# A landmark attention with a two-layer MLP on one core: from hand-woven generators to pieces of work ordered by an in-kernel list scheduler, with DMA transposes in turn with the loads and stores in four parts

## The chip, the cores and the metric

The kernel runs on one core of one Trainium2 chip. The metric is the device time of one execution in microseconds (us), the lower the better. A profile of one execution goes with each kernel; its span is the time from the first to the last instruction, some 2 us shorter than the device time of the same run. A run whose time is more than 1.5% above the fastest of the same kernel counts as slow; comparisons use fast runs only.

PE is TensorE's matmul, PEld its weight load, ACT is ScalarE, DVE is VectorE, POOL is GpSimd, SP is SyncE, which here only starts DMAs.

## The reference

The attention compares each of 576 tokens with 32 landmarks (means of 18 tokens each) instead of all tokens, for 8 batches of 8 heads; a two-layer MLP with Silu between its layers follows. Cut to what matters:

```python
q, k, v: (8, 8, 576, 64)            # batch, heads, tokens, head size
q_lm = q.reshape(B, H, 32, 18, D).mean(axis=3)      # k_lm likewise
A  = softmax(scale * q @ k_lm.T)     # 576 x 32
Bm = softmax(scale * q_lm @ k_lm.T)  # 32 x 32
C  = softmax(scale * q_lm @ k.T)     # 32 x 576
Z = Bm.T / (norm1(Bm) * norminf(Bm) + 1e-6)
for _ in range(6):
    Z = 2 * Z - Z @ Bm @ Z           # Newton's iteration for an inverse
x = (A @ Z @ C @ v)                  # heads side by side: (4608, 512)
h = x @ w_in                         # w_in (512, 2048)
return (h * sigmoid(h)) @ w_out      # w_out (2048, 512)
```

Both kernels fold Z, C, v and w_in into one matrix per batch, m = (Z C v) w_in, so that the first layer is A times m and its input never exists as such.

## The kernel before

All matmuls go through one helper, which is why most PE rows of its profile have line 60. Here are the parts that the change touches, with cuts marked.

```python
# landmark sums: 18 matmuls against an identity, 256 columns each
for j in range(J):
    mm(lmv, idb, qk[:, :, :, j, :], start=(j == 0), stop=(j == J - 1))
# transposes of q and k, on DVE, in 32x32 blocks
nc.vector.transpose(out=qT[:, 0, g]..., in_=qk[:, 0, g]...)
# landmarks spread over a block diagonal, so that a 128-row weight serves four heads
nc.vector.tensor_tensor(out=lmbd, in0=bc(lmT, 4, 2), in1=bc(hmask, 8, 1), op=OP.mult)
# scores of A and C: full 128-row products, most of whose weight is zero
mm(sa[:, hf, 0:HS2], LB(1, g, c), qT[:, 0, g, c, ...], start=(c == 0), stop=(c == 1))
mm(c_ps[0:VP, ...], kt[:, c, i], LB(0, g, c), start=(c == 0), stop=(c == 1))
# row sums of A: a product of 4 columns, reciprocal, a transpose, a product that spreads it
mm(csv[0:c1 - c0, ci, 4*g:4*g + 4], ets[g][:, c0:c1], honesb)
...
# first layer, with Silu as h/2 * (1 + tanh(h/2)): ACT does tanh, DVE the rest
mm(h_ps[:, hf, 0:HS2], m_t[b][:, g, dc*128:(dc+1)*128], etn_t[b][:, g, ...], ...)
nc.scalar.activation(out=sig, in_=h_ps[:, :, 0:HS2], func=AF.Tanh, scale=0.5)
nc.vector.scalar_tensor_tensor(out=gT[:, dc, o:o + S]..., in0=sig, scalar=1.0,
                               in1=h_ps[:, :, 0:HS2], op0=OP.add, op1=OP.mult)
...
# second layer; one store for all token rows of a batch that an output tile holds
mm(ops, gT[:, dc, c*128:(c+1)*128], w_out_sb[:, dc, :], start=(dc == 0), stop=(dc == NDC-1))
nc.scalar.activation(out=ost, in_=ops, func=AF.Copy, scale=0.5)
nc.sync.dma_start(out=out[b*S:(b+1)*S, :].rearrange("(l j) n -> j l n", j=J)[j:j+n],
                  in_=ost[p0:p0 + n * L, :])
...
# the order: attention is a generator with 26 stops, taken in equal steps between MLP units
for i, u in enumerate(units):
    want = (i + 1) * NST // len(units)
    while done < want:
        done += 1
        next(gen, None)
    u()
```

The softmax here doesn't subtract the row's maximum and nothing guards it: scores larger than these inputs give would overflow.

## Time and profile before

| | before |
|---|---|
| device time, median of 4 runs | 316.17 us (314.15 to 316.33) |
| span of the profiled run, mean granted clock | 312.8 us, 0.984 |
| PE, ACT, DVE, GpSimd busy | 90%, 53%, 66%, 10% |
| first matmul of the first layer | 34.9 us |
| last matmul starts | 305.0 us |

The prediction below shows the lines of the page and of the waits. One more view helps: the table of windows, which gives the length of each stretch, the busy time of each engine in it with the number of instructions in brackets, the granted clock, and the mean share of the 16 DMA engines that was busy (the times of the packets added up, so it can pass 1).

```profile
core 0: us, PE busy (x) PEld busy (x) DVE busy (x) ACT busy (x) POOL busy (x), PEclk, DMA share, GB/s
0.00:35.00 35.00, 16.16 (x175) 11.16 (x176) 26.15 (x60) 9.55 (x15) 15.92 (x30) 0.92 1.05 188
35.00:65.00 30.00, 25.55 (x241) 15.94 (x240) 26.19 (x53) 17.41 (x30) 4.93 (x8) 0.98 1.02 175
...
100.00:260.00 160.00, 159.05 (x1322) 91.31 (x1321) 109.34 (x223) 97.53 (x163) 8.02 (x13) 1.00 0.30 62
```

The reader is to see two things. In the first 35 us PE is busy for 16 while DVE is busy for 26. From 65 us on PE is busy nearly all the time, and the DMA engines have little to do: a share of 0.30 from 100 to 260 us. So there is room on DMA and GpSimd for work that PE and DVE do.

A busy PE isn't yet a PE at its rate: a matmul's row has its length with the pipeline in it (379 ns), while eight in a row start every 216 ns. So I call **PE work** the number of matmuls of each form times the distance at which that form follows itself in the trace, and for tiled forms one pass shared by the tiles that run at once. What is left of a stretch is **lost**; matmuls on zeros count as lost. Before: 253.0 us of work and 59.8 lost, of 312.8.

### The profile page before, as it was taken

The numbers are of one execution on the slowest core, as the hardware profiler recorded it, in microseconds if no ns is written. First come the engines' busy times: TensorE is split into PE (matmuls) and PEld (weight loads), VectorE is DVE, ScalarE is ACT, GpSimd is POOL, SyncE is SP. The second block draws the span as 40 slices with busy tenths as digits, with TensorE's granted clock in tenths as the row PEclk, the third lists the DMA queues.
The fourth block names the chain that finished last, engine by engine and source line by source line (L and its number), as shares of the span: only waits on it lengthen the run. The fifth ranks groups of instructions, "written<-read, shape, count | busy, mean of one in ns | idle before, by whom it ended". The sixth has DMA issues, their size and how long they took to land.

```text
span 312.8 us, 5645 instructions
## 1 busy us (share of the span) xinstructions
PE 280.7 (90%) x2268; PEld 161.9 (52%) x2268; DVE 207.4 (66%) x420; ACT 166.8 (53%) x277; POOL 32.0 (10%) x55
## 2 busy tenths in 40 slices
PE   0465889979999999999999999999999999999990
PEld 0443464546555654666455744665465644555440
DVE  6857689998988697579747794676448664555000
ACT  1042664775466665765475646565645757555110
POOL 7342302100210020102001020000000000000000
PEclk9998699999999999999999999999999999999997
DMA  6999999672528152193418261110111101121122
GB/s 116 210 209 207 206 210 209 86 147 69 96 50 151 56 91 56 45 161 62 83 55 145 73 90 46 52 24 16 35 55 36 44 11 45 47 47 56 52 77 75
DMA packets 18379, 28.16 MB, mean 90 GB/s; under 512 B 944, under 2 KB 9136, under 8 KB 18352
## 3 DMA queue, kind: packets, MB, share of 16 engines
q0 software_dynamic: 13600, 18.35, 34.6%
q1 hardware_dynamic: 4752, 9.44, 10.8%
q8 instruction: 18, 0.29, 0.4%
q14 instruction: 9, 0.07, 0.1%
HBM read 36.70 MB, written 9.44 MB: 147 GB/s over the span
## 4 chain that ended last, share of the span: by engine, by line
PE 72%; DVE 11%; DMA 8%; ACT 4%; issue 2%; POOL 1%; POOLq 0%; ACTq 0%
PE ops L60 36%; PE h_ps L60 18%; DVE gT L393 5%; DMA v_97<-in_v_dram 4%; PE lm_ps L60 3%; DMA w_in_sb<-in_moe_w_in_dram 3%; PE m_ps L60 3%; PE c_ps L60 2%; ACT sig L391 2%; PE w_ps L60 2%; PE sa_ps L60 2%; PE ns_ps L60 2%; DVE qT L171 2%; PE rb_ps L60 1%; ACT m L377 1%
## 5 line engine op out<-in xcount | busy, mean ns | idle before, releaser
L60 PE MATMUL ops<-w_out_sb,gT 128*128 128x512 bf16 x576 | 150.6, 379 | 0.1
L393 DVE SCALAR_TENSOR_TENSOR gT<-sig,h_ps 128x576 bf16<-128x576 bf16 x128 | 94.8, 746 | 53.2 <-ACT sig L391 53.0
L391 ACT ACTIVATE sig<-h_ps 128x576 bf16<-128x576 f32 x128 | 82.4, 651 | 56.9 <-PE h_ps L60 54.4
L60 PE MATMUL h_ps<-etn,m 128*128 128x288 bf16 x512 | 84.3, 287 | 3.4 <-DVE gT L393 2.6
L60 PEld LDWEIGHTS <-gT 128*128 128x128 bf16 x576 | 52.5, 98 | 44.3 <-issue 6.3
L60 PEld LDWEIGHTS <-m 128*128 128x128 bf16 x512 | 47.9, 98 | 34.6 <-issue 11.6
L377 ACT CAST m<-m_ps 128x1024 bf16<-128x1024 f32 x32 | 32.1, 1019 | 14.2 <-PE m_ps L60 14.1
L409 ACT ACTIVATE ost<-ops 128x512 f32<-128x512 f32 x36 | 21.4, 598 | 21.8 <-PE ops L60 21.6
L60 PE MATMUL lm_ps<-qk,idb 128*128 128x256 bf16 (+1 forms) x162 | 22.2, 289 | 6.3 <-DVE sel L127 6.3
L171 DVE STREAM_TRANSPOSE qT<-qk 128x576 bf16<-128x576 bf16 x32 | 23.8, 755 | 1.6 <-PE c_ps L60 1.6
L239 DVE SCALAR_TENSOR_TENSOR st<-st,ns_ps 128x320 bf16<-128x320 bf16 (+1 forms) x48 | 20.7, 432 | 5.5 <-PE ns_ps L60 5.4
L60 PEld LDWEIGHTS <-idb 128*128 128x128 bf16 x162 | 16.2, 112 | 11.2 <-issue 6.8
L166 DVE STREAM_TRANSPOSE qT<-qk 128x1152 bf16<-128x1152 bf16 x16 | 21.7, 1354 | 0.0
L304 ACT ACTIVATE ct<-c_ps 96x768 bf16<-96x768 f32 x16 | 12.9, 806 | 7.5 <-PE c_ps L60 7.5
L60 PE MATMUL ns_ps<-st 128*128 128x160 bf16 (+1 forms) x96 | 13.7, 223 | 2.1 <-DVE st L239 1.4
L60 PE MATMUL m_ps<-w_in_sb,zt 64*32 64x512 bf16 x256 | 13.8, 414 | 1.8 <-ACT m L377 1.0
L60 PE MATMUL c_ps<-lmbd,qT 128*96 128x128 bf16 x192 | 14.2, 219 | 0.2 <-ACT et L256 0.2
L60 PEld LDWEIGHTS <-qT 128*96 128x96 bf16 x192 | 13.3, 123 | 1.9 <-issue 0.4
L159 ACT CAST lm<-lm_ps 128x256 bf16<-128x256 f32 x8 | 3.0, 375 | 20.3 <-PE lm_ps L60 20.3
L290 DVE TENSOR_TENSOR etn<-et,rb_ps 128x576 bf16<-128x576 bf16 x16 | 12.0, 748 | 1.9 <-PE rb_ps L60 1.8
L256 ACT ACTIVATE et<-sa_ps 128x576 bf16<-128x576 f32 x16 | 10.4, 648 | 3.9 <-PE sa_ps L60 3.8
L73 POOL DMA_DIRECT2D qk<-in_k_dram x8 | 5.8, 720 | 62.3 <-PE lm_ps L60 45.4
(78 smaller groups left out, 171.4 us busy)
## 6 DMA issues: line engine op xcount, KB each, us to landing
out_dram<-ost SPq DMA_DIRECT2D x32, 256.0 KB
qk<-in_k_dram POOLq DMA_DIRECT2D x8, 576.0 KB, 5.6
qk<-in_q_dram POOLq DMA_DIRECT2D x8, 576.0 KB, 8.9
v_96<-in_v_dram POOLq DMA_DIRECT2D x12, 192.0 KB, 6.4
v_97<-in_v_dram POOLq DMA_DIRECT2D x12, 192.0 KB, 6.6
w_out_sb<-in_moe_w_out_dram POOLq DMA_DIRECT2D x4, 512.0 KB, 16.1
w_in_sb<-in_moe_w_in_dram POOLq DMA_DIRECT2D x2, 512.0 KB, 11.1
w_in_sb<-in_moe_w_in_dram POOLq DMA_DIRECT2D x4, 256.0 KB, 12.2
```

The source lines that it names most:

```text
L60: nc.tensor.matmul(out=out_ap, lhsT=lhsT, rhs=rhs, start=start, stop=stop, skip_group_check=True)
L73: nc.gpsimd.dma_start(out=qk[:, t].rearrange("p g j d -> p g (j d)"), in_=src[b].rearrange("(g h) (l j) d -> (h l) g (j d)", g=NG, l=L))
L166: nc.vector.transpose(out=qT[:, 0, g].rearrange("p c j l -> p j c l"), in_=qk[:, 0, g].rearrange("p j (c x) -> p j c x", c=2))
L171: nc.vector.transpose(out=qT[:, 1, g, c].rearrange("p (i a) l -> p a i l", a=VA), in_=qk[:, 1, g].rearrange("p (a i) (c x) -> p a i c x", ...
L239: nc.vector.scalar_tensor_tensor(out=st2[:, :, lo:SW], in0=st[:, :, lo:SW], scalar=2.0, in1=ns_ps[:, 0:NG * SW].rearrange("p (g x) -> p g ...
L256: nc.scalar.activation(out=et.rearrange("p (f x) -> p f x", f=2), in_=sa[:, :, 0:HS2], func=AF.Exp, scale=sc / J)
L290: nc.vector.tensor_tensor(out=etn[:, g, :].rearrange("p (f x) -> p f x", f=2), in0=ets[g].rearrange("p (f x) -> p f x", f=2), in1=rb[:, :, ...
L304: nc.scalar.activation(out=ct.rearrange("p (f x) y -> p f (x y)", f=2), in_=c_ps[0:VP, :, 0:384], func=AF.Exp, scale=sc / J)
L377: nc.scalar.copy(out=m_sb[:, :, f * 512:(f + 1) * 512], in_=m_ps)
L391: nc.scalar.activation(out=sig, in_=h_ps[:, :, 0:HS2], func=AF.Tanh, scale=0.5)
L393: nc.vector.scalar_tensor_tensor(out=gT[:, dc, o:o + S].rearrange("p (f x) -> p f x", f=2), in0=sig, scalar=1.0, in1=h_ps[:, :, 0:HS2], op ...
L409: nc.scalar.activation(out=ost, in_=ops, func=AF.Copy, scale=0.5)
```

## The change

The intent is to take work off PE and DVE, give it to DMA, GpSimd and ACT, and find an order in which nothing waits. Every piece of work (some matmuls, one copy, one load) becomes an object with a duration, what it depends on, a priority and the PSUM banks that it needs (PSUM holds what matmuls write, in eight banks). A list scheduler in the kernel's source goes through time and gives each engine the ready piece of the best priority. The order of instructions on each engine is then fixed.

The parts, beside the order:

- q and k are transposed by DMA from batch 2 on (by PE in batches 0 and 1); landmarks are summed by GpSimd from batch 2 on;
- scores of A and C run as 64-row by 32-column tiles, eight at once, without the block diagonal;
- row sums of A come from one product with a block of ones, which also spreads them; Ln and Exp on ACT take the reciprocal;
- C is computed with landmarks as rows, so its sums come out of the exponential; it is transposed by DMA (by PE in batches 0 and 1);
- Silu is one instruction on ACT, with a table load at each change between Silu and Exp;
- transposes wait until two of three v loads of the batch have landed, and loads wait for the transposes of the batch before;
- an output tile is stored by four DMAs of 64 KB;
- matmuls on zeros keep PE running in the first 45 us.

The diff, cut to its core:

```diff
+class Op:
+    def __init__(self, name, engs, emit, deps=(), prio=0.0, psum=0, cls=None, table=None,
+                 tiled=False, dma=0.0, lag=None, group=None, crit=False):
...
+class Plan:
+    LAG = {"PE": 0.24, "ACT": 0.17, "DVE": 0.12, "POOL": 0.2, "SP": 1.6}
+    MARGIN = 0.4
+    WARM = 45.0
...
+                    for o in cand[e]:
+                        r = o.ready + o.margin
+                        if r > t + 1e-9: ... continue
+                        if best is not None and o.prio >= best.prio:
+                            continue
+                        if e == "ACT" and o.table == "silu" and group[0] is not None:
+                            continue
...
+                    if e == "PE":
+                        if o.tiled != tiled[0]:
+                            dur += 0.08
...
+def act_us(n): return 0.06 + 0.00083 * n
+def dve_us(n): return 0.07 + 0.00104 * n
+def mm_us(n, count=1): return count * max(n / 2400 + 0.0025, 0.028)
...
-                nc.vector.transpose(out=qT[:, 0, g]..., in_=qk[:, 0, g]...)
+            gate = v_ops[b][-2:-1]
+                    qt_ops[t, g] = [A(f"xt{t}{g}.{b}", [("SP", 1.38)],
+                        lambda e, t=t, g=g: nc.sync.dma_start_transpose(
+                            out=qT[:, t, g], in_=qk[:, t, g].rearrange("p j d -> p (j d)")),
+                        [qk_ops[b, t]] + use + gate, p0 + 5, lag=XLAG)]
...
-                mm(lmv, idb, qk[:, :, :, j, :], start=(j == 0), stop=(j == J - 1))
+                xs = [pool(f"la{g}", 576, s1[:, g], src[:, g, 0:9], src[:, g, 9:18],
+                           [qk_ops[b, t], tree[0]]) for g in range(NG)]
+                x = pool("lb", 512, s2, s1[:, :, 0:4], s1[:, :, 4:8], xs)
+                x = pool("lc", 256, s1[:, :, 0:2], s2[:, :, 0:2], s2[:, :, 2:4], [x])
...
-                mm(sa[:, hf, 0:HS2], LB(1, g, c), qT[:, 0, g, c, ...], ...)
+            def am(e, g=g):
+                for h in range(4):
+                    for c in range(2):
+                        mm(bank(me[f"A{g}"], c)[L * h:L * h + L, 0:HS],
+                           lmT[64 * c:64 * c + 64, 1, g, L * h:L * h + L],
+                           qT[64 * c:64 * c + 64, 0, g, :, L * h:L * h + L])
...
-        nc.scalar.activation(out=sig, in_=h_ps[:, :, 0:HS2], func=AF.Tanh, scale=0.5)
-        nc.vector.scalar_tensor_tensor(out=gT..., in0=sig, scalar=1.0, in1=h_ps..., ...)
+                               lambda e, dc=dc, cell=cell: nc.scalar.activation(
+                                   out=gm[:, dc, :], in_=bank(cell["o"]), func=AF.Silu),
...
+    def later_loads(b):
+        p = last[b - 2]
+        gate = last[b - 1]["xts"][-2:-1] if b > NPE else []
+        if b - 2 >= NPE:
+            gate = gate + last[b - 2]["cts"][:1]
+        load_qk(b, 100.0 * b - 150, p["qk_read"], gate)
+        load_v(b, 100.0 * b - 149, [p["cv"]], gate)
...
-                    out=out[b*S:(b+1)*S, :].rearrange("(l j) n -> j l n", j=J)[j:j + n],
-                    in_=ost[p0:p0 + n * L, :])
+            eng.dma_start(
+                out=out[b*S:(b+1)*S, c0:c1].rearrange("(l j) n -> j l n", j=J)[j],
+                in_=ost[L * n:L * n + L, c0:c1])
```

## The prediction

> **What bounds the kernel now.** I read the page first: the line of busy time by engine, then the forty slices.
>
> ```profile
> PE 280.7 (90%) x2268; PEld 161.9 (52%) x2268; DVE 207.4 (66%) x420; ACT 166.8 (53%) x277; POOL 32.0 (10%) x55
> ...
> PE   0465889979999999999999999999999999999990
> PEld 0443464546555654666455744665465644555440
> DVE  6857689998988697579747794676448664555000
> ACT  1042664775466665765475646565645757555110
> ```
>
> PE is full from the tenth slice on; DVE is at eight or nine tenths in slices 7 to 13 and drops later. The waits agree: PE waits little for others, while ACT and DVE wait for PE.
>
> ```profile
> ACT sig L391 <- PE h_ps L60: 54.4, 63, 2.8
> DVE gT L393 <- ACT sig L391: 53.0, 57, 2.2
> ...
> PE lm_ps L60 <- DVE sel L127: 6.3, 1, 6.3
> ...
> PE h_ps L60 <- DVE gT L393: 2.6, 5, 1.2
> ```
>
> So the bound is PE, except at both ends. But busy PE is not PE at its rate, so I priced its work by spacing. The timeline shows "PE ops x8" in 1.73 us, 216 ns each; "h_ps x8" in 0.98 us, 123 ns; twelve c_ps in 0.67 us, 56 ns; nine lm_ps in 0.98 us, 109 ns; ten cs_ps of width 4 in 0.39 us, each lasting 164 ns, so 25 ns apart. A small matmul with a full weight load can therefore follow each 25 ns. Times the counts of these groups:
>
> ```profile
> L60 PE MATMUL ops<-w_out_sb,gT 128*128 128x512 bf16 x576 | 150.6, 379 | 0.1
> L60 PE MATMUL h_ps<-etn,m 128*128 128x288 bf16 x512 | 84.3, 287 | 3.4 <-DVE gT L393 2.6
> L60 PE MATMUL lm_ps<-qk,idb 128*128 128x256 bf16 (+1 forms) x162 | 22.2, 289 | 6.3 <-DVE sel L127 6.3
> L60 PE MATMUL c_ps<-lmbd,qT 128*96 128x128 bf16 x192 | 14.2, 219 | 0.2 <-ACT et L256 0.2
> ```
>
> second layer (ops) 576 x 0.216 = 124.4; first layer (h_ps) 512 x 0.1225 = 62.7; lm 15.7 (126 x 0.109 and 36 narrow ones at 0.056); c 10.7; sa 64 x 0.1225 = 7.8; m 256 in concurrent eights, 32 x 0.216 = 6.9; w 192 x 0.04 = 7.7; ns 6.0; sums and their spreading (cs, rt, rb) 8.0; the rest 2.8. **PE's work is 252.7 us of a 312.8 us span.** The other 60 us, from the counts in windows: 25 before the first h_ps at 35.1 us (about 10 us of work done by then); 12 in 35 to 100; 13 in 100 to 260 (8%, gaps between unlike pieces); 2 after; 7.4 from the last matmul at 305.4 to the end, for one copy and one store.
>
> The chain of waits in the first 36 us shows the start:
>
> ```profile
> 4.90 10.16 DMA w_in_sb<-in_moe_w_in_dram
> 15.34 13.71 DMA v_97<-in_v_dram
> 29.77 0.70 PE m_ps L60 x5
> 30.49 1.94 ACT m L377 x2
> 33.10 2.04 PE lm_ps L60 x9
> 35.13 0.96 PE h_ps L60 x4
> ```
>
> The timeline says more than the DMA labels: the landmark sums start only at 12.50, held by DVE's constants (two memsets of 2.62 us, then sel), and attention 0 runs serially from there, each of its Newton steps taking 0.9 us.
>
> **What the Trainium skill says.** "TensorE: Matmul & The Clock Gate", section "Back-to-back issue gap", gives N/2.4 + 2.5 ns warm: 216 ns at 512. The trace agrees (1.73 us for eight). "ScalarE: Activation LUTs", section "What ACT_TABLE_LOAD costs", gives 1283 ns plus a drain of 1380 per switch; the trace has one load, of 1.28 us, and no switch, so the drain is not seen here. "GPSIMD Engine Reference", section 3.1, measures about 2.6 cycles an element for a two-input add, at 1.2 GHz; no run here has one. "DMA: Bandwidth & Descriptors", section "Latency and other measured facts", has DMA transposes at 261 GB/s (350 to 400 contiguous); none here yet.
>
> **The change, part by part: PE.** Both layers keep their columns: the second 72 x 0.216 = 15.5 us a batch; the first becomes 32 matmuls of 512 and 32 of 64, 6.9 + 32 x 0.029 = 7.8. That is 23.4, as before. Attention, per batch, before and after:
> - landmark sums 2.0, now six adds per tensor on GpSimd (batches 0 and 1 stay on PE); four small transposes of the landmarks, 0.2, are added;
> - C scores 1.3 and A scores 1.0 become 64-row by 32-column tiles, eight at once: 0.25 each, say 0.5 with the change of tiling;
> - row sums 1.0 become four 288-column products with a block of ones, 0.5 (reciprocal by Ln and Exp on ACT);
> - C times V loses its ones columns: 192 to 128 columns, 1.0 to 0.7;
> - Newton 0.75, m 0.9 (say 1.1), zt and the rest 0.6.
>
> Sum after: 23.4 + 4.9 = about 28.3 a batch, against 31.6. Batches 0 and 1 pay 4.7 more each (36 sums, 36 transposes, 12 of C). **8 x 28.3 + 9.4 = about 235.5 us, 17 less than before.** Warm-up matmuls only fill time in which PE has nothing else.
>
> **DVE and ACT.** DVE loses its transposes (23.8 + 21.7 us), lmbd 5.5 and the 94.8 us of gT; what is fixed on it sums from the old rows to about 7 us a batch (chain and Newton 5.5, two etn at 0.75). ACT's Silu takes 18 x 0.60 = 10.8 us (the row of ost, 598 ns at 512 columns); exponentials and logarithms twelve of 288 columns at 0.40 and three others, 6.4; two table switches at 2.66, 5.3 by the skill: 22.5. Copies that either takes, 9. Together 38.5 over two engines, 19 each, under PE's 28: **neither is the bound on average**, though in an exponential stage Silu has to wait.
>
> **DMA and GpSimd.** Transposes move 128 x (4 x 1152 + 2 x 768) x 2 bytes = 1.57 MB a batch, 6 us at the skill's 261 GB/s (an estimate); loads 0.88 MB and stores 1.18 MB at the 207 GB/s of the page's early slices, 10. That is 16 us of some 29, even with loads and transposes in turn. GpSimd: 4608 elements at 2.2 ns, 10 us (an estimate from that page), and five load issues, 3.2 (rows of 720 and 588 ns): 13 of 29. Both hidden.
>
> **Start.** K lands near 7 us as now, q near 9; sums 1 us each, warm; landmark transposes, scores and the exponential with its table 3 to 4; the chain to f0 2; six Newton steps with the two groups in turn at 0.7, 4; zt, m and its copy 1.7. First h_ps near 22 instead of 35. The copies and transposes of batch 1 run beside this: about 12 us of work done, **10 lost instead of 25**. From 22 to 45 Silu of batch 0 (10.8 us against PE's 7.8) and w_out's late landing cost perhaps 5 (was 12).
>
> **Steady part.** Pieces of the second layer (four matmuls, 0.86 us) fill whatever attention leaves, and PE takes an attention piece only 0.4 us after it is ready. I take 5% lost of the remaining 218, 11 us; before it was 8%.
>
> **End.** The last block comes in two halves whose stores go out in four parts from two queues: 5 instead of 7.4.
>
> Sum: 235.5 + 10 + 5 + 11 + 5 = 266.5 us of span, and 3.4 for the difference between timed runs and span before (316.18 against 312.8): about 270. I add 2 for gaps at the many changes of tiling: **272 us**.
>
> **Rivals.** (1) ACT becomes the bound: its order is Silu or exponentials, never mixed, and no exponential stage may start with a first layer open. For it: 22.5 us fixed and up to 9 of copies is 31, above PE's 28, if DVE takes few; DVE is also quick to stall a chain. Against: the order is planned so that either engine takes a copy when free. It would make the period 31 to 33 us, and 290 to 300 in all. (2) Transposes with their turns arrive late: each batch passes load, wait, transpose, wait, and a fixed order can't step around a late one, so PE stands before the scores. For it: six transposes, five loads and eighteen stores share a period. Against: 16 of 29 us. At 2 us a batch for six batches: 284. (3) PE's old loss of 8% stays, as it comes of PE's own switching and not of order: 6 us more, 278. (4) The start is even better hidden and the steady loss 2%: 260.
>
> **Range and chances.** Work of 235 to 240 is the surest term; the losses of 20 to 50 us on top of it make the range: 258 to 289. For a result within 2% of now, 40 us of it would have to be given back by a new wait; chances 0.94 faster, 0.04 same, 0.02 slower.
>
> **What will show it.** PE's matmuls of 512 columns 216 ns apart; first first-layer matmul near 22 us (right: 19 to 25); PE idle in total under 20 us after that; ACT under nine tenths in the steady slices, with 16 or so table loads; DVE under half busy; the DMA share below eight tenths after slice 8; end of matmul to end of span about 5 us. Wrong would be: PE waiting for scores behind a transpose, ACT full while PE waits for Silu, or GpSimd adds several times longer than estimated, holding back the landmarks.

## The result

| | before | after |
|---|---|---|
| device time, median of 4 runs | 316.17 us | 276.88 us (274.86 to 277.45) |
| span, mean granted clock | 312.8 us, 0.984 | 275.0 us, 0.994 |
| PE work | 253.0 us | 228.4 us |
| lost in the span | 59.8 us | 46.6 us |
| first matmul of the first layer | 34.9 us | 30.7 us |
| last matmul starts, span ends | 305.0, 312.8 us | 270.5, 275.0 us |
| ACT, DVE, GpSimd busy | 53%, 66%, 10% | 64%, 35%, 39% |

The ratio of after to before is 0.876, with a 95% interval of 0.872 to 0.880. A ratio here is the mean time of one kernel's fast runs over that of the other's fast runs of the same rounds, so it isn't quite the ratio of the medians. The time is inside the predicted range of 258 to 289 us, 4.9 us above the predicted 272.0.

The page after, with the lines that answer to those of before:

```profile
PE 261.1 (95%) x2383; PEld 133.0 (48%) x2383; DVE 96.2 (35%) x261; ACT 176.4 (64%) x403; POOL 107.3 (39%) x133
...
PE   8999999997989989996999999999999999999993
...
ACT  1689697559884889985389898769881391111120
...
DMA  6999999999999899986999999543002321323223
```

PE is full from the first slice on, but the first slices are the matmuls on zeros. ACT works at eight or nine tenths in many slices of the middle, for at most five slices on end. DMA is near nine tenths to slice 25, where before it fell after slice 7. And in the last third ACT has little to do: the last product m starts at 198.6 us, so attention is through, and from 226 to 271 us only second layer is left.

Groups of instructions of after, by line, engine, form, count, then busy time and mean ns of one:

```profile
L811 ACT ACTIVATE gm<-ps 128x512 bf16<-128x512 f32 x128 | 67.0, 631 | 4.0 <-PE ps L323 3.7
...
L516 POOL TENSOR_TENSOR sa<-qk 128x576 f32<-128x576 bf16 x24 | 31.0, 1310 | 16.6 <-DMA qk<-in_k_dram 16.1
```

Silu takes 631 ns for 512 columns, one instruction in place of two. GpSimd's adds of 576 elements take 1310 ns, 2.27 ns an element. The second layer keeps its distance of 216 ns.

The waits, as engine and line, what it waited for, total us, times, longest:

```profile
POOL sa L516 <- DMA qk<-in_k_dram: 16.1, 6, 4.8
...
PE ps L323 <- DMA ct<-ce: 3.7, 2, 2.5
```

The chain that ended last, followed in order of time (start us, us, what); I show the start, the longer of two waits for a transpose of C, and the end:

```profile
6.35 14.56 DMA w_in_sb<-in_moe_w_in_dram
21.19 6.12 DMA w_in_sb<-in_moe_w_in_dram
...
126.14 2.73 DMA ct<-ce
...
171.54 93.59 PE ps L323 x655
...
269.28 1.62 DMA out_dram<-ost
```

Three things are to be seen. The first 27 us hang on w_in, which is still landing. Twice PE waits for a transpose of C (ct), 3.7 us in all. And from 171.5 us on the chain is PE alone for 94 us, up to the last copies and stores.

**Where the time came from.** By the same count of starts and distances, the span fell by 37.9 us, of which 24.6 are PE work and 13.2 are lost time:

| PE work, us | before | after |
|---|---|---|
| second layer and first layer | 187.1 | 187.3 |
| landmark sums (after: batches 0 and 1 only) | 15.7 | 4.0 |
| scores of A and C | 18.5 | 4.6 |
| row sums of A and their spreading | 8.0 | 3.9 |
| C times v | 7.7 | 5.1 |
| transposes of q, k, landmarks and C on PE | 0 | 7.1 |
| m, Newton and the rest | 16.0 | 16.4 |

| lost, us | before | after |
|---|---|---|
| to the first matmul of the first layer | 25.7 | 17.7 |
| from there until attention is through (after: 200 us, before: 260) | 26.1 | 23.6 |
| from there to the last matmul | 0.3 | 0.8 |
| last matmul to the end of the span | 7.8 | 4.5 |

The landmark sums and the transposes were tried by runs below. The scores, whose work fell most, the row sums and Silu as one instruction were not: their part is a count from the traces.

The middle hardly gained: after loses 14% of it. I sorted it by what stands at each gap of PE, with each pass of the tiles charged whole. From 45 to 200 us of after, some 11 of 22.5 us are 110 gaps at a change between untiled and tiled matmuls (or between two tilings), 6.9 us are four waits of over 0.6 us each, and the other 4 or so are small gaps within and between pieces of the same tiling. In the middle of before, 112 changes cost some 12 us, other gaps 10 and waits 4.0. So the order did part of what it was to do, and took more than half of the gaps between like pieces away; changes cost as much as before in a shorter middle, and waits grew. Between full and 64-by-32 matmuls a change costs 0.09 us on the way to the tiles and 0.10 on the way back: from the last tile of 512 columns to the next full matmul are 0.318 us, of which its pass takes 0.216, and for 288 columns 0.225, of which 0.122.

### The profile page after: what moved, and what is told of

It reads as the page before. It is cut to its first block, busy times and chain, and to the rows that moved or that the text cites. A ratio compares the mean times of both kernels' runs of the same rounds, so it can differ in the third digit from the quotient of the medians.

```text
span 275.0 us, 6159 instructions
## 1 busy us (share of the span) xinstructions
PE 261.1 (95%) x2383; PEld 133.0 (48%) x2383; DVE 96.2 (35%) x261; ACT 176.4 (64%) x403; POOL 107.3 (39%) x133
## 4 chain that ended last, share of the span: by engine, by line
PE 71%; DMA 11%; ACT 9%; DVE 3%; POOL 2%; issue 2%; SPq 0%; POOLq 0%; ACTq 0%; DVEq 0%
PE ps L323 71%; DMA w_in_sb<-in_moe_w_in_dram 8%; ACT gm L811 4%; DMA ct<-ce 2%; DMA out_dram<-ost 1%; POOL qk L368 1%; ACT m L333 1%; ACT L923 1%; DVE bm L570 1%; ACT ln L658 1%; ACT ost L333 1%; DVE etn L667 1%; POOL v L375 1%; ACT gx L834 1%; DVE m L335 0%
## 5 line engine op out<-in xcount | busy, mean ns | idle before, releaser
L323 PE MATMUL ps<-w_out_sb,gm 128*128 128x512 bf16 x512 | 121.8, 381 | 0.0
L323 PEld LDWEIGHTS <-gm 128*128 128x128 bf16 x512 | 47.4, 98 | 52.4 <-issue 3.5
L811 ACT ACTIVATE gm<-ps 128x512 bf16<-128x512 f32 x128 | 67.0, 631 | 4.0 <-PE ps L323 3.7
L323 PE MATMUL ps<-etn,m 128*128 128x64 bf16 (+1 forms) x512 | 69.3, 286 | 0.0
L516 POOL TENSOR_TENSOR sa<-qk 128x576 f32<-128x576 bf16 x24 | 31.0, 1310 | 16.6 <-DMA qk<-in_k_dram 16.1
L620 DVE SCALAR_TENSOR_TENSOR st<-st,ps 128x320 bf16<-128x320 bf16 (+3 forms) x54 | 21.4, 405 | 20.2 <-PE ps L323 18.3
L335 DVE CAST m<-ps 128x512 bf16<-128x512 f32 x32 | 20.3, 685 | 9.7 <-PE ps L323 9.7
L516 POOL TENSOR_TENSOR sb<-sa 128x512 f32<-128x512 f32 (+1 forms) x24 | 21.9, 912 | 1.9
L333 ACT CAST m<-ps 128x512 bf16<-128x512 f32 x32 | 17.5, 609 | 3.5 <-PE ps L323 3.4
L323 PE MATMUL ps<-w_out_sb,gx 128*128 128x512 bf16 (+1 forms) x80 | 16.3, 336 | 0.3 <-ACT ost L333 0.3
L667 DVE TENSOR_TENSOR etn<-et,ln 128x576 bf16<-128x576 bf16 x16 | 14.3, 893 | 1.8 <-ACT ln L662 1.8
L323 PEld LDWEIGHTS <-st 128*128 128x128 bf16 x96 | 8.1, 98 | 10.3 <-DVE st L620 1.1
## 6 DMA issues: line engine op xcount, KB each, us to landing
v<-in_v_dram POOLq DMA_DIRECT2D x24, 192.0 KB, 10.7
```

Source lines behind the costliest of these rows:

```text
L323: nc.tensor.matmul(out=out_ap, lhsT=lhsT, rhs=rhs, start=start, stop=stop, skip_group_check=True)
L333: nc.scalar.copy(out=out, in_=in_)
L335: nc.vector.tensor_copy(out=out, in_=in_)
L516: lambda e: nc.gpsimd.tensor_tensor(out=o_, in0=a_, in1=b_, op=OP.add),
L620: nc.vector.scalar_tensor_tensor(out=s2[:, g0:g1, lo:SW], in0=s[:, g0:g1, lo:SW], scalar=2.0, in1=ps[:, 0:NG * SW].rearrange("p (g x) -> p ...
L667: nc.vector.tensor_tensor(out=etn[:, g, :], in0=et.rearrange("p c x -> p (c x)"), in1=ln.rearrange("p c x -> p (c x)"), op=OP.mult)
```

## The experiments

My theory after the result had four parts. PE's work is still the price of nearly everything. The order is what keeps the moved work from stalling PE. Transfers are now close behind as a second limit, so the turns and the four-part stores matter. The changes of tiling are a true cost, about 0.11 us each. The rivals: that attention's own pace through the transfers is the bound and PE only fills the time; that any sensible order would do; that the turns and four-part stores are decoration, as DMA had room before; that the gaps at the changes are only waits for data put down wrongly.

Every run was correct except the first, which is wrong. Ratios are to the kernel before in the same rounds; after stands at 0.876.

### Half the second layer (wrong result)

```diff
-                    mm(ps, src(dc), w_out_sb[:, dc, c0:c1], start=(dc == 0), stop=(dc == NDC - 1))
+                    if dc % 2 == 0:
+                        mm(ps, src(dc), w_out_sb[:, dc, c0:c1], start=(dc == 0), stop=(dc == NDC - 2))
```

> Half of the second layer's matmuls left out (a wrong result on purpose): 288 of 576 at 216 ns, 62 us of PE work. If PE's work alone sets the time of the changed kernel, 277 falls by 62 to about 215 us. If the attention stages have a pace of their own (24 us a batch from 30 to 200 us in the trace, the DMA queues nine tenths busy), the last first-layer piece still comes near 215 to 225 us and the total stays at 225 to 235 us.

Measured: 235.95 us, ratio 0.747 (0.744 to 0.750). It skips half the second layer, 62 us of PE work, and returned 41. PE lost about 45 us between 30 and 180 us instead of 22 (up to 5 of it matmuls missing from the trace, 25 of 2087): there the other 21 went. The page has the slices of PE and DMA:

```profile
PE   8999999977799888899986588899998999999990
...
DMA  5999999999999999897987996999897630112554
```

PE shows fives to eights in many slices of the middle, and DMA is near nine tenths to slice 29. What says most is the start of m in the eight batches: 25.1, 58.6, 90.7, 105.9, 140.1, 154.2, 185.1 and 198.6 us in after, and 25.8, 55.5, 88.7, 104.2, 140.9, 154.9, 186.2 and 199.4 here. Attention goes at the same pace with a good part of PE's other work gone. So attention has a pace of its own in this order (whether transfers or dependences set it isn't shown), and PE's second layer fills what it leaves. What doesn't fit is done afterwards: that is the pure second layer at after's end. The rival that attention's pace is the bound is wrong for after, where some 70 us of PE's work are left when attention is through. But work taken out doesn't pay in full either: here a third of it came back as idle PE in the middle, though some 17 us of second layer and 8 of first were still left after attention. The time, 236 us, is at the upper end of the second expectation, 225 to 235.

### All transposes and landmark sums back on PE

```diff
-    NPE = 2
+    NPE = 8
```

(With it, two dependences that the reuse of buffers then needs, and the condition under which later loads are made.)

> All eight batches take their transposes and landmark sums on PE, none by DMA transpose or GpSimd: 6 x 84 more matmuls of 128 columns at 56 ns, 28 us of PE work more, and no turn-taking of transfers. If PE's work sets the time: 277 + 28 less the 7 us of long waits = 298 to 305 us. If the attention's pace through DMA and GpSimd cost PE more than those waits, the loss is smaller: 280 to 292 us. DVE's bm (404 ns) and etn (893 ns) should fall back to the 224 and 748 ns of the kernel before if it is GpSimd's adds that slow them.

Measured: 299.81 us, ratio 0.950 (0.946 to 0.955), 22.9 us above after. The edit adds 28 us of PE work (36 sums, 36 transposes and 12 of C in each of six batches). Waits of over 0.6 us fell from 6.9 to 1.6 us in the middle, so about 5 came back. The time followed PE's work nearly one for one: the first part of the theory holds. The same run settled a side question, as it has no GpSimd adds at all. One group of DVE, in after first and then in this run:

```profile
L570 DVE TENSOR_TENSOR bm<-pb,pbs 128x64 bf16<-128x64 f32 x8 | 3.2, 404 | 0.3
```

```profile
L570 DVE TENSOR_TENSOR bm<-pb,pbs 128x64 bf16<-128x64 f32 x8 | 1.8, 223 | 0.2
```

Without GpSimd's adds this instruction is as fast as in the kernel before (224 ns). The product etn goes from 893 to 753 ns likewise (748 before). So the adds slow DVE beside them. In after two of the eight bm instructions ran beside an add: they took 0.57 and 1.31 us, and each ended 0.08 us after its add did, as if it had waited for the add's end. The other six took 0.225.

### No turns between transposes and loads

```diff
-            gate = v_ops[b][-2:-1]
+            gate = []
```

(And the same in the loads and in the transposes of C.)

> The turns of transfers taken away: transposes and loads may run at once, only the buffers' own dependences stay. If the turns are what made attention wait (POOL waited 19 us for transposes, SP 37 us for v): 2 to 6 us faster, 271 to 275. If transposes beside loads get slower by more than the turns cost: landings over 3.6 us (transposes of qT) and 2.8 us (ct), same or slower, 277 to 285. If PE's work hides both: within 1 us.

Measured: 290.18 and 292.12 us in its two fast runs, ratio 0.922 (0.915 to 0.929); two more runs, 297.8 and 299.4, count as slow. That is about 15 us above after, on the fast runs. The view of the tile qT on SP gives the time from issue to landing as least, median and most, after first and then this run:

```profile
DMA to landing us min/median/max: 3.3/3.6/5.0
```

```profile
DMA to landing us min/median/max: 3.2/6.2/18.3
```

One transpose without turns took 18.3 us to land, and four issued together held SP for 14.3 us instead of 5.7 to 7.0. Transposes of C, which PE waits for, had a median of 4.4 instead of 2.8 us. PE lost about 20 us between 60 and 100 us, against 7.5 in after (30 matmuls are missing from that trace). The scheduler's plan is also a little different when these dependences are gone, so not each of the 15 us is proved to be the landing itself; that the landing is slower is shown. The direction was expected, the size was not: 285 us was the most.

### The kernel before with GpSimd's landmark sums, in its own order

```diff
+            for g in range(NG):
+                add(s1[:, g], src[:, g, 0:9], src[:, g, 9:18])
+            add(s2, s1[:, :, 0:4], s1[:, :, 4:8])
...
+        elif b >= 2:
+            yield
```

> The kernel before with one part of the change alone: the landmark sums of batches 2 to 7 as GpSimd adds, its order left as it is. PE loses 108 matmuls of 256 columns at 109 ns, 11.8 us. If PE's work sets its time too: 316 - 12 = 304 us. If GpSimd's adds slow DVE (which is two thirds busy there[...]) or its loads come late behind the adds, less: 308 to 316 us.

Measured: 329.64 us, ratio 1.044 (1.039 to 1.049): 13.5 us slower, though 12 us of PE work are gone. Waits of this run:

```profile
PE sb_ps L60 <- DVE lmbd L204: 10.7, 2, 9.0
...
DVE lmT L202 <- POOL lm L153: 7.3, 2, 5.5
```

The sums come late, DVE's transpose waits for them in its fixed place, and PE waits behind DVE for up to 9.0 us. DVE also waits 3.4 us for q and k, whose later loads GpSimd issues behind the adds; in before it waits for none. Both expectations, 304 and 308 to 316 us, missed, as neither had a loss. Between 35 and 100 us PE lost 35.5 us instead of 11.8. So moving work off PE alone can be a loss when the order was made for another place of the work.

### The same pieces, but a plan with wrong durations

```diff
     def add(self, *a, **k):
         o = Op(*a, **k)
+        o.engs = [(e, 0.5) for e, d in o.engs]
```

> The scheduler told that every piece takes 0.5 us on every engine; dependences, priorities and banks as they are. If the calibrated durations are what the order is worth, the in-order engines wait for each other and the time goes to 300 us or more. If the priorities do it (attention first, second layer as filler) and durations matter little: under 285.

Measured: 333.43 us, ratio 1.055 (1.048 to 1.061). All dependences, buffers and priorities are those of after; only the plan believes that each piece takes half a microsecond. It costs 56.6 us. The waits of over 0.6 us sum to 40.2 us in twenty places, against 6.9 in four. Two rows of its waits carry most of it:

```profile
PE ps L324 <- POOL lm L517: 15.6, 3, 6.9
PE ps L324 <- DMA ct<-ce: 15.2, 7, 9.0
```

A list scheduler isn't good by itself: with wrong durations it is slower than the hand-woven order. With its durations wrong the whole gain is gone; those of after are close to what the trace shows: the plan takes 0.485 us for a Silu of 512 columns and 1.40 for a GpSimd add of 576, and in after four Silus in a row take 2.06 us and the add 1.31.

### One DMA for each store

```diff
-        ost_st[i] = [A(f"os@{prio}", [("SP", 2.2)],
-                       lambda e: [store(e, n) for n in range(4)], [c], prio, dma=0.65, lag=1.5)]
+        def store_all(e):
...
+                r = nc.sync.dma_start(
+                    out=out[b * S:(b + 1) * S, c0:c1].rearrange("(l j) n -> j l n", j=J)[
+                        j:place[m][1] + 1:step],
...
+            ost_st[i] = [A(f"os@{prio}", [("SP", 0.55 if place[0][0] == place[3][0] else 1.1)],
+                           lambda e: store_all(e), [c], prio, dma=0.65,
```

> Stores in one part (the last block excepted): one issue per 128 rows, two for a block of two batches, instead of four. If four parts are only a cost to SP (140 issues at 0.43 us, 60 us of SP, ahead of transposes in its queue), one part is 1 to 4 us faster. If a store in one part lands later or slower and holds up ost, or the transposes behind it: slower by 1 to 4 us. If stores are hidden: within 1 us.

Measured: 303.94 us, ratio 0.963 (0.958 to 0.968), 27 us above after; all three expectations, none of over 4 us either way, missed. The table of windows of this run, in the tail where nothing but stores runs on DMA (the columns are as above, the share of DMA is the last but one; the next three microseconds read 0.26, 0.25 and 0.25):

```profile
288.50:289.50 1.00, 1.00 (x8) 0.61 (x7) 0.00 (x0) 0.12 (x1) 0.00 (x0) 1.00 0.25 86
```

A share of 0.25 is four of sixteen engines. The Trainium skill, "DMA: Bandwidth & Descriptors", section "Why a DMA increments its semaphore by 16 and not by 1", says that the number of engines is the largest up to 16 that divides the slowest dimension of both sides; that dimension is 4 on the side of out in this store (128 on the other), so 4 engines, and the trace agrees. In four parts the slowest dimension is 32. A store of 256 KB takes 6.24 us in this run at its end; one of 64 KB takes 1.7 us, with a share of up to 0.59 in after's tail. But the end of the span grew by 3 us only. The waits of PE of over 0.6 us grew from 6.9 to 21.6 us in the middle, and they are for others behind the stores:

```profile
POOL sa L516 <- DMA qk<-in_k_dram: 35.8, 6, 7.4
...
PE ps L323 <- DMA ct<-ce: 13.7, 5, 4.4
```

My reading is that a load or a transpose over all sixteen engines is done only when the four that also hold a store's packets are, so each store delays whatever runs beside it; no view here shows single engines. The plan is another one too, as a store takes less of SP's time in it. What is shown is that k and q land in 10.5 and 13.3 us instead of 6.3 and 9.5, GpSimd waits 35.8 us for k, and PE 13.7 for the transpose of C.

A wait of PE can cost more than its length. In this run the granted clock falls to 0.5 five times before the last matmul, for 3.4 or 6.8 us, each time 1.8 to 4.3 us after the start of a PE wait of 2.2 to 4.5 us, and matmuls of 512 columns then start 426 ns apart instead of 216. I estimate some 7 of the 27 us from the matmuls that are slower so. PE stood at half clock for 3.4 us in after, 27 here, 38 in the run with GpSimd's sums in the old order, and 58 with wrong durations.

### The kernel before with stores in four parts

```diff
-                n = min(4 * c + 4 - jj, J - j)
+                n = 1
```

> The kernel before with one part of the change alone: each store in parts of 32 rows (144 of 64 KB). In the changed kernel with stores in one part the DMA share was 0.25 during a store, 4 of 16 engines, and the time 304 instead of 277 us. If it is the four engines that cost, in the kernel before the last store lands 3 us earlier (6.6 us now): 312 to 313 us, and no more, since PE there does not wait for transfers after 60 us. If stores on four engines also delayed its loads and their waits reach PE: 305 to 311.

Measured: 313.26 us, ratio 0.992 (0.988 to 0.995): 2.7 us. All of it is the end: from the last matmul to the end of the span are 5.0 us instead of 7.8, and the lost times of the stretches before are within 0.5 us of those of before. The same part is worth 27 us in after and 3 here. That fits the kernel before, in whose middle PE never waits for a transfer and the DMA share is 0.30.

### Fewer changes of tiling

A of both groups, C of both groups, and m in pairs are joined into one piece each, from batch 2 on.

```diff
-            def am(e, g=g):
-                for h in range(4): ...
+            def am(e, gs=range(NG) if of else (g,)):
+                for g in gs:
+                    for h in range(4): ...
```

> The changed kernel with its tiled pieces joined in pairs from batch 2 on: both groups' A scores in one piece, both C scores, and the four m pieces in two; the same matmuls. In its trace each change between the whole array and 64x32 tiles costs PE 0.09 us going in and 0.21 coming out, and all 138 changes of tiling cost 20 us. If that is a cost of the change itself, some 20 to 30 changes fewer save 3 to 4 us: 273 us. If it is the wait for the pieces around, or if the larger pieces wait for four free PSUM banks, nothing is saved or up to 6 us are lost: 277 to 283.

Measured: 272.97 us (272.43 to 274.97), ratio 0.866 (0.862 to 0.870), 3.9 us below after by the medians. But the trace has 133 changes of tiling against 138, and they cost 14.7 us against 14.9; the plan had placed many of those pieces side by side already. So the edit didn't try what it was made for. It is faster, and the waits fell to 6.2 us, but what made the rest of the gain isn't shown: I put it down to the luck of another order, and the expected 273 us was met by luck too. (The 0.21 us and 20 us in the expectation charged most of a tiled pass to the way back; the change itself costs 0.10 there.)

### The cost of a change of tiling by itself

In the tail, where PE runs the second layer only and nothing else can be waited for, eight 64-by-32 matmuls of 32 columns on zeros are put in after each of 24 pieces.

```diff
+                if prio >= SW_FROM:
+                    for h in range(4):
+                        for c in range(2):
+                            mm(banks[c][L*h:L*h + L, 0:L], zer[64*c:64*c + 64, 0:L],
+                               zer[64*c:64*c + 64, 0:L])
```

> A measurement of the change of tiling by itself: in the changed kernel after each of the 24 second-layer pieces of the last batch, in the stretch where PE does nothing else and loses 0.4 us in 66, eight 64x32 matmuls of 32 columns on zeros (results unused; their own spacing 3 ns, 0.05 us together). If going to another tiling and back costs 0.30 us as such: 24 x 0.35 = 8 us more, 285 us. If the 0.30 us read in the trace is waiting for other engines: 1 to 2 us more, 278 to 279.

Measured: 281.22 us (280.32 to 283.64), ratio 0.892 (0.887 to 0.897), 4.3 us above after. The timeline of PE in that stretch:

```profile
258.43 1.04 PE L324 MATMUL ps<-w_out_sb,gm 128*128 128x512 bf16 x4
259.40 0.21 PE L324 MATMUL ps<-zer 64*32 64x32 bf16 x8
259.54 1.04 PE L324 MATMUL ps<-w_out_sb,gm 128*128 128x512 bf16 x4
```

Four full matmuls alone repeat every 0.864 us (four times 0.216). Here the period is 1.11 us, so one excursion to the tiles and back costs about 0.24 us. By the starts, 92 ns are extra on the way in, the eight tiles start within some 25 ns, and from the last of them to the next full matmul it is 0.12 us, some 25 ns of that the tiles' own pass. The last matmul starts 5.5 us later than in after, as 23 such returns make it. There is no data to wait for here, so the gaps at changes are a cost of PE itself: that rival fell. The middle of after agrees, once a tiled pass is charged whole: 0.09 us there and 0.10 back. The size was between the two expectations, of 8 us and of 1 to 2.

### The input weights before batch 1

```diff
-    load_qk(1, -95)
     load_v(0, -90)
     for f in range(4):
         load_w_in(f, -80 + f)
+    load_qk(1, -60)
```

> The first loads in another order: w_in ahead of batch 1's q and k. In the changed kernel the first-layer matmuls begin at 30.7 us, held by w_in, which lands behind 1.18 MB of batch 1 at some 205 GB/s (5.8 us). If w_in's landing bounds the start, they begin near 25 us; of that, as batch 1's work then comes later, 1 to 3 us reach the end: 274 to 276. If PE is only re-ordered, the same time; if batch 1's later attention holds PE up in 35 to 60 us, slower, up to 281.

Measured: 276.67 us, ratio 0.877 (0.873 to 0.881), no change. The first matmul of the first layer comes at 25.2 instead of 30.7 us, as w_in lands sooner. But PE's lost time from 7 us to 30.7 is 10.9 us against 10.7: in after this wait was filled with batch 1's sums and transposes, which now come later. An earlier milestone isn't an earlier end when PE had other work.

### No matmuls on zeros

```diff
-    WARM = 45.0
+    WARM = 0.0
```

> The changed kernel without its 95 warm-up matmuls. If they only keep PE's clock up for work that waits for w_in anyway (landing at 27 to 30 us), PE's clock falls in the first 30 us and the time stays within 1.5 us of 277. If the cold clock lengthens the first attention (12 us of work) beyond w_in's landing: 280 to 285.

Measured: 272.77 us (271.61 to 273.64), ratio 0.864 (0.860 to 0.867), 4.1 us faster than after. Both of my expectations missed. The timelines of PE, this run first and then after, show the cold start:

```profile
7.10 2.08 PE L323 MATMUL ps<-qk,idb 128*128 128x128 bf16 x18 [7.10 <-DMA qk<-in_k_dram]
```

```profile
7.00 1.17 PE L323 MATMUL ps<-qk,idb 128*128 128x128 bf16 x18
```

The first 36 such matmuls take 3.8 us instead of 2.0, starting 107 to 110 ns apart instead of 56. Yet the first layer starts at 28.1 instead of 30.7 us, and PE loses 16.6 us to 30.7 instead of 17.7. The filling matmuls stand in the order like any others, and pieces that become ready wait behind them. The plan after 45 us is another one too (3.5 us lost from 100 to 140 us against 7.2), so how much of the 4 us is the filling and how much the order isn't settled.

### Joined pieces, six output buffers, and stores as four pieces

```diff
-    ost_r = ring(outp, [128, DMODEL], FP, "ost", 3)
+    ost_r = ring(outp, [128, DMODEL], FP, "ost", 6)
...
-            ost_st[i] = [A(f"os@{prio}", [("SP", 2.2)], ... all four stores ...)]
+            ost_st[i] = [A(f"os{n}@{prio}", [("SP", 0.55)], ... store n ...) for n in range(4)]
```

> The joined pieces of the run before (273.0 us) and two more edits: six ost buffers instead of three, and the four stores of a block as four separate pieces of SP's order, so that a transpose can go between them (in the changed kernel four stores of 3.0 us stood before the two ct transposes for which PE then waited 2.65 us). If stores in SP's queue are what made ct late, the long waits of 6 to 7 us halve and the time is 269 to 271 us. If the waits come of durations that the order did not foresee, the order only moves: 272 to 276.

Measured: 275.54 us (274.42 to 276.58), ratio 0.872 (0.869 to 0.875): better than after by about 1 us, worse than the joined pieces alone by 2.6. The waits for the transpose of C fell from 3.7 to 2.0 us as intended. But attention came later (the last m at 214.5 instead of 198.6 us). So this was a miss, and it shows the size of what I can't control: an edit of a few dependences moves the result by 2 to 4 us through the order alone.

The fastest versions measured are the one without matmuls on zeros (272.77 us) and the one with joined pieces (272.97), both faster than either kernel. They were not tried together.

## Why the prediction was right, and where its steps were not

The total was right within 2%, but by steps whose errors cancelled in part, and that is luck. Its terms against the trace, in us:

| term of the sum | predicted | measured | error |
|---|---|---|---|
| PE work | 235.5 | 228.4 | -7.1 |
| lost to 45 us (10 at the start, 5 up to 45) | 15 | 18.8 | +3.8 |
| lost from 45 us to the last matmul (11, and 2 for changes of tiling) | 13 | 23.3 | +10.3 |
| last matmul to the end | 5 | 4.5 | -0.5 |
| span to device time | 3.4 | 1.7 | -1.7 |
| **sum** | 271.9 | 276.7 | +4.8 |

The measured column is the profiled run, of 276.66 us. The 3.4 was a misreading: it set a median of 316.18 us beside the span of another run. Where time and span are of the same run, they differ by 1.7 to 2.4 us in every run.

- **PE work as the price** was right, and shown by the run with all transposes on PE (+22.9 us for 28 us of work). The sum was 7 us too high, mostly since it gave 0.5 us for each batch's A and C and 1.1 for m, while they took 0.58 for A and C together and 0.85 for m.
- **The start** failed as a step: "First h_ps near 22 instead of 35". It was 30.7, outside the 19 to 25 that I had named as right. The reason is in the loads. The step "loads 0.88 MB" (a batch) was wrong by half: q and k are 576 KB each and v three times 192 KB, 1.77 MB. With w_in behind batch 1's q and k, its last part landed after 27 us, at a rate of 205 GB/s that was full. The error in time was less than in the milestone (17.7 us lost at that point instead of 10, but 1.1 up to 45 us instead of 5), since batch 1's work filled the wait. The run with w_in first shows that: milestone 5.5 us earlier, same time.
- **"the DMA share below eight tenths after slice 8"** was wrong for the same reason: it is 0.93 to 1.01 from 66 to 180 us. Six such batches leave no spare transfers, which is why the turns (15 us) and the four-part stores (27 us) weigh so much here. The second rival, late transposes, was right in kind, for a few waits of up to 2.65 us, not in size.
- **"I add 2 for gaps at the many changes of tiling"** is the term most mis-sized. All 138 changes took about 15 us. Another 5 or so were hidden in the high prices of A, C and m, so about 7 of the 15 were foreseen, in two places. The inserted tiles show that the cost is real.
- **"I take 5% lost"** of the steady part: without the changes of tiling it was about right (6.9 us of waits and some 4 of small gaps), with them it was 14% up to 200 us. The third rival, "PE's old loss of 8% stays, as it comes of PE's own switching and not of order", named the mechanism.
- **ACT and DVE off the bound** was right: 64% and 35% busy, and PE's longest wait for ACT is 1.9 us. The sign named for it, "ACT under nine tenths in the steady slices", was not met: nine slices of ACT read 9. I expected 16 or so table loads; there were 11 of 1.28 us, as the plan shares stages between batches. So the first rival, ACT as the bound, fell.
- **GpSimd's adds** took about 5.9 us for each of q and k, against 5 estimated; 39% busy. They didn't hold back the landmarks much (one wait of 2.06 us), as the plan knew their durations.
- **"Warm-up matmuls only fill time in which PE has nothing else"** was not so: without them the first layer began 2.6 us sooner and the time was 4.1 us less, in part by another order.
- **The end** was right: 4.5 us against 5.

What the prediction didn't ask is what the order itself is worth. The plan with wrong durations (+57 us) and the moved sums in the old order (+13.5 us) say that without it the same pieces would have been slower than before.

## What to carry to other kernels

When work is moved off the bound engine, the order has to move with it: give a scheduler durations measured from the kernel's own profile, and check that PE's lost time sorts into waits and switches. Once the middle depends on transfers, their shape counts: a store on four engines and a transpose between loads each cost more in what stood behind them than in themselves, and long waits of PE were followed by stretches at half clock. Count changes of tiling as work, about 0.2 us for there and back, and don't put matmuls on zeros into an order without measuring it without them.

## What the Trainium skill lacked or had wrong

- "TensorEngine Tiling (Array Packing)", section "Key Properties": it says that a change of mode drains TensorE and gives no time. Here it was 0.09 us to 64-by-32 tiles and 0.10 back, beyond the pass of the tiles; 138 changes took about 15 us of a 275 us span.
- "DMA: Bandwidth & Descriptors", section "Rules for kernel authors": "A transpose next to ordinary DMAs needs nothing". All results were correct here too, but without turns the median landing of a transpose went from 3.6 to 6.2 us and the longest from 5.0 to 18.3, and the kernel took 15 us more.
- "DMA: Bandwidth & Descriptors", the section on the semaphore's 16: the rule for the number of engines agrees (a share of 0.25 for an outer dimension of 4). The page doesn't say of such a store that it delays others that use all sixteen (of loads beside another kind of traffic it does say so): q's landing went from 9.5 to 13.3 us.
- "GPSIMD Engine Reference", section "8. Key points": it names contention with DVE instructions that have two inputs in SBUF, and the traces agree. That section has no size; another page of the skill goes further, so this is a gap of the section only. Here, with GpSimd's adds, the mean of one form went from 223 to 404 ns, and of another from 753 to 893; the instructions beside an add took up to 1312 and 1814 ns.
- "ScalarE: Activation LUTs", section "What ACT_TABLE_LOAD costs": 1283 ns agrees in all 11 loads. The drain of 1380 ns didn't show here: the timeline has the load right after the Silu before it, and the exponential right after the load.

```profile
118.23 0.62 ACT L834 ACTIVATE gx<-ps 128x512 bf16<-128x512 f32 x1
118.85 1.28 ACT L923 ACT_TABLE_LOAD   x1
...
120.14 0.22 ACT L561 ACTIVATE pb<-ps 128x64 f32<-128x64 f32 x1
```
